# Regrouping the lead-in of a fused linear-attention and gated feed-forward kernel

## The chip, the cores and the metric

The kernel runs on one core of one Trainium2 chip. The metric is the device time of one execution in microseconds (us); less is better. The time before is 211.69 us, the median of 7 runs, from 210.19 to 416.03 us; the six runs other than the longest lie between 210.19 and 212.92 us.

## The reference

Linear attention with a decay per head, in blocks of 64 positions, and after it a feed-forward layer whose gate is `h * cos(h)`:

```
q, k, v: (4, 8, 768, 64) f32     lam: (8,)     w_in: (512, 2048)     w_out: (2048, 512)
for each block b of 64 positions (sl):
    intra = (q[sl] @ k[sl].T * Dmask) @ v[sl]          # Dmask = lam ** (i - j), 0 above the diagonal
    inter = (q[sl] * lam ** (pos + 1)) @ kv_state
    out[sl] = intra + inter
    kv_state = lam ** 64 * kv_state + (k[sl] * lam ** (63 - pos)).T @ v[sl]
x = out as (3072, 512)            # tokens by heads * head_dim
h = x @ w_in
g = h * cos(h)
return g @ w_out                  # (3072, 512) f32
```

## The kernel before

The 3072 tokens are 24 blocks of 128, numbered n from 0. They are gathered into eight feed-forward tiles of 4, 2, 2, 2, 2, 4, 4 and 4 blocks (`TILES`). The decay is put into q and k/v as powers of lam beforehand (`q_sp`, `v_sp`, `q_scale`, `v_scale`), so that a block needs only a masked product and a running state.

**The first tile, blocks 0 to 3, is the lead-in.** It has a code path of its own, `add_span(x)`, for x = 0 and 1; each x stands for 256 positions of one batch entry, two tokens to a partition. For each x the loads bring 512 KB of q, k and v (`sp_f`). The eight heads are handled in two halves, hp = 0 and 1. For each half: q and v are scaled to bf16 (`prep`, line 475), k is cast (`prep_k`, line 479), q and k are transposed on TensorE (line 486) and evicted (line 489), the scores are formed (line 497) and masked (line 502), and the values are multiplied in (line 523). Between the two blocks of one x lies the state: `update` (line 510) forms k times v, `update_out` (line 514) brings it to `kv_bd`, `carried` (line 529) adds it to the second block, and `values_out` (line 537) evicts a block into `xT`, the transposed input of the feed-forward.

**A feed-forward tile** (`add_ffn`) has 16 chunks f of 128 hidden columns. `hidden` (line 591) does four matmuls a chunk into `ps_h`, ScalarE takes the cosine (line 597), VectorE multiplies (line 603) into `g`. For tile 0 the first `SPLIT` chunks are done in two halves, blocks 0 and 1 and then blocks 2 and 3, so that work can begin before the last `xT` is there. Then `project` (line 631) multiplies `g` by w_out: for each block j four groups of four matmuls of 512 columns, called by their first chunk f0 = 0, 4, 8 and 12; the group f0 needs quarter f0/4 of w_out. The finished block is evicted (line 643) and stored (lines 650 and 652).

**The later blocks** come through `prepare` (scaling at lines 323 and 331, cast of k at line 327), transposes on TensorE (line 351) for blocks 4 and 5 and by DMA (line 357) from block 6 on, `add_scores` (line 384) and `add_stretch` (state at line 412, values at lines 424 and 428). Their work is laid between the groups of the feed-forward of the tile before.

**The weights** are cast from f32 to bf16 by DMAs that GpSimd issues (line 264): w_in in pieces of `W_IN` chunks, w_out in four quarters. `ORDER` gives the order of all loads: q, k and v of x = 0 and 1, then w_in, then w_out, then the loads of block 4 and on. The first w_in piece is issued when k of x = 1 has landed, and the load of q of block 4 waits until the third quarter of w_out has landed:

```python
ORDER = "q0 k0 q1 k1 v0 v1 i0 i1 i2 i3 i4 o0 o1 o2 o3"
W_IN = [3, 3, 4, 3, 3]
        deps = [kept[-3 if soft else -2]] if at and (names[at - 1][0] in "io") != soft else []
```

**The order on every engine is fixed when the program is built.** A planner (`Planner.order`) plays the tasks through with a cost for each and picks, engine by engine, the task that can start first and, of those, the one of lowest priority number. The instructions are then written out in order of planned start; an engine runs them strictly in that order, and where the chip is later than the plan it waits. The costs that matter here: 0.5 us on SyncE for the issue of a load, 0.8 us on GpSimd for that of a weight piece, 2.6 us of DMA for four chunks of weights, 1.5 us for a load of `sp_f`, 1.1 us for one of a later block, and 1.6 to 2.8 us from the end of a transfer until its data may be used:

```python
    SETUP = {"POOL": 5.6, "DVE": 5.6, "ACT": 7.3, "SP": 1.3}
    MM = lambda cols, n=1: n * (cols / 2400.0 + 0.0025)
        _, w_t[which, c] = dma("POOL", 2.6 * part, 0.8, emit, ...)
                    t = pl.add("PE", MM(width, U4), ..., project, pr, banks=0 if f0 else 1)
```

Where the plan leaves TensorE idle in the lead-in, `keep_awake` writes out matmuls on a blank tile (line 706); it stops at the chunk `lead_end = hid[2 * SPLIT]`.

Of the kernel before, what the change touches and what calls it, by code (L numbers as in the profile page):

```python
# [18 lines left out]
SPANS = 2  # L19
DMA_FROM = 6  # L20
TILES = [4, 2, 2, 2, 2, 4, 4, 4]
SPLIT = 4
BANKS = 7
LAG = 2
ATT = 0.95
ALONE = [2, 3, 4]

QV = [[("DVE", "POOL"), ("DVE", "POOL")], [("DVE", "POOL"), ("DVE", "POOL")]]
OUTS = [{"qT": ("DVE", "DVE"), "kT": ("ACT", "ACT")}, {"qT": ("ACT", "ACT"), "kT": ("ACT", "ACT")}]
V_PRIO = {"POOL": -1.7, "DVE": 0.0}  # L30
LATE = 30.0
ORDER = "q0 k0 q1 k1 v0 v1 i0 i1 i2 i3 i4 o0 o1 o2 o3"

W_IN = [3, 3, 4, 3, 3]


class Task:
# [101 lines left out]
def kernel(  # L139
# [10 lines left out]
    nc = tc.nc  # L150
    B, H, S, D = q.shape
    P = 128
    NB = S // P
    NBLK = B * NB
    NP = H // 2
# [3 lines left out]
    KF = D_FF // P  # L159
# [33 lines left out]
    for i in range(2):  # L193
        m = mask_sp[i * D:(i + 1) * D].rearrange("u k (s t) -> u k s t", s=2)
# [24 lines left out]
    v_sp = consts.tile([P, H, 2], F32)  # L219
# [179 lines left out]
    def add_stretch(pr):  # L399
# [59 lines left out]
        for x, y in zip(chain, chain[1:]):  # L459
            x.then = y  # L460
            y.deps.append(x)

    def add_span(x):
# [3 lines left out]
        us = {"DVE": 0.69, "POOL": 1.1}  # L467
# [4 lines left out]
        place = lambda t, hp: t[:, :, cut[hp]].rearrange("u s h d -> u h s d")  # L472

        def prep(_, name, hp, e):
            vec[e].tensor_mul(place(L[name], hp), live[name + "_f", "sp", x][:, cut[hp]],  # L475
                              (q_sp if name == "q" else v_sp)[:, cut[hp]].unsqueeze(3).to_broadcast([P, 4, 2, D]))

        def prep_k(_, hp):
            nc.scalar.copy(place(L["k"], hp), live["k_f", "sp", x][:, cut[hp]])

        def transposes(task, name, hp):
            t = L["t", name, hp] = bank(task.bank[0], [P, 2, 2, P], BF16, "ps_t")
# [50 lines left out]
        def values_out(_, c, e, pairs):  # L533
# [3 lines left out]
            (nc.scalar.copy if e == "ACT" else nc.vector.tensor_copy)(  # L537
                live["xT", 0][:, pairs, n * P:(n + 1) * P], L["o"][c][:, pairs])

        so, kt, v_t = [[], []], [], []  # L540
        for hp in range(2):
            eq, ev = QV[x][hp]
            a = pl.add(eq, us[eq], [load_t["q_f", "sp", x]], partial(prep, name="q", hp=hp, e=eq), pa(-0.9 + 0.1 * hp))
            kt.append(pl.add("ACT", 0.61, [load_t["k_f", "sp", x]], partial(prep_k, hp=hp), pa(-0.9 + 0.1 * hp)))
            v_t.append(pl.add(ev, us[ev], [load_t["v_f", "sp", x]], partial(prep, name="v", hp=hp, e=ev), pa(V_PRIO[ev] + 0.1 * hp)))
            outs = []
            for name, src in (("qT", a), ("kT", kt[hp])):
                e = OUTS[x][name][hp]
                t = pl.add("PE", MM(P, 4), [src], partial(transposes, name=name, hp=hp), pa(-0.5 + 0.1 * hp), banks=1)
                outs.append(pl.add(e, 0.58 if e == "ACT" else 0.42, [t], partial(transposes_out, name=name, hp=hp, e=e), pa(-0.5 + 0.1 * hp)))  # L550
                t.bank_frees = [[outs[-1]]]
            s1 = pl.add("PE", 0.42, outs, partial(scores, hp=hp), pa(0.1 + 0.1 * hp), banks=2)
# [19 lines left out]
    h_last, o_last = {}, {}  # L572
    hid = []

    def add_ffn(i):
# [4 lines left out]
        for f in range(KF):  # L580
            gate[f] = []
            blocks = [(0, 2), (2, 4)] if i == 0 and f < SPLIT else [(0, nb)]
            for b0, b1 in blocks:
# [16 lines left out]
                def gated(_, f=f, at=at, n=n):  # L600
                    if ("g", i) not in live:
# [4 lines left out]
                h = pl.add("PE", MM(n, 4), [x for m in range(n0 + b0, n0 + b1) for x in Vo[m]] + [w_t["in", next(c for c in range(len(W_IN)) if f < sum(W_IN[:c + 1]))]],  # L606
                           hidden, pr, banks=1)
                a = pl.add("ACT", 0.21 + n * 0.000833, [h], cosine, pr, get="cos")
                d = pl.add("DVE", 0.12 + n * 0.00104, [a] + ([o_last[i - 2]] if i >= 2 else []), gated, pr)
# [8 lines left out]
        for j in range(nb):  # L618
# [3 lines left out]
            for piece, part in enumerate(pieces):  # L622
                width = part.stop - part.start
                for f0 in range(0, KF, U4):
                    pr = begins[i + 1] + (j + f0 / KF) * nxt / nb + piece

                    def project(task, j=j, f0=f0, piece=piece, part=part, width=width):
                        if f0 == 0:
                            live["f", i, j, piece] = bank(task.bank[0], [P, DM], F32, "ps_f")
                        for f in range(f0, f0 + U4):  # L630
                            nc.tensor.matmul(live["f", i, j, piece][:, :width], lhsT=live["g", i][:, f, j * P:(j + 1) * P],  # L631
                                             rhs=w_out_sb[:, f, part], start=(f == 0), stop=(f == KF - 1))
# [35 lines left out]
    for at, name in enumerate(names):  # L668
        which, n = name[0], int(name[1:])
        soft = which in "io"  # L670
        deps = [kept[-3 if soft else -2]] if at and (names[at - 1][0] in "io") != soft else []
        if soft:
            kept.append(add_w({"i": "in", "o": "out"}[which], n, at, deps))
        elif n < SPANS and at < 15:
# [70 lines left out]
```

## The time and the profile before

| what | value |
|---|---|
| median of 7 runs | 211.69 us |
| the profiled execution, its own time | 211.13 us |
| span of the profile, first to last instruction | 209.4 us |
| TensorE busy (matmuls) | 199.0 us, 95% of the span |
| VectorE, ScalarE, GpSimd busy | 120.3, 112.1, 63.6 us |
| mean granted TensorE clock | 0.992 |
| first matmul of the feed-forward (line 591) | at 16.99 us |
| first matmul of the projection (line 631) | at 32.90 us |
| first transpose of block 4 (line 351) | at 39.20 us |

In the profile's lines PE is TensorE (matmul), PEld its weight loads, DVE is VectorE, ACT is ScalarE, POOL is GpSimd, SP is SyncE; a q behind the name is the engine's sequencer, which waits and issues DMAs. A line of the timeline gives start, duration, engine, line of the program, operation, `out<-in` with its shape and count, and in brackets the idle time of the engine just before it and what ended that.

### The profile page before, as it was taken

The numbers are of one execution on the slowest core, as the hardware profiler recorded it, in microseconds if no ns is written. First come the engines' busy times: TensorE is split into PE (matmuls) and PEld (weight loads), VectorE is DVE, ScalarE is ACT, GpSimd is POOL, SyncE is SP. The second block draws the span as 40 slices with busy tenths as digits, with TensorE's granted clock in tenths as the row PEclk, the third lists the DMA queues.
The fourth block names the chain that finished last, engine by engine and source line by source line (L and its number), as shares of the span: only waits on it lengthen the run. The fifth ranks groups of instructions, "written<-read, shape, count | busy, mean of one in ns | idle before, by whom it ended". The sixth has DMA issues, their size and how long they took to land.

```text
span 209.4 us, 4536 instructions
## 1 busy us (share of the span) xinstructions
PE 199.0 (95%) x1786; PEld 116.8 (56%) x1813; DVE 120.3 (57%) x220; ACT 112.1 (54%) x207; POOL 63.6 (30%) x82
## 2 busy tenths in 40 slices
PE   6769999999999999999999999999999999999993
PEld 6448544447856758766664555445445444444462
DVE  3695773274975849676849797838533444333000
ACT  5967875325917737656545745654554555355120
POOL 4099000164335726363636554610000000000000
PEclk9996999999999999999999999999999999999999
DMA  4999999998999999999999999931101110111112
GB/s 127 347 240 142 185 206 221 209 241 227 211 215 210 277 191 263 199 248 203 267 247 213 246 260 231 229 106 48 50 1 49 53 52 0 50 50 50 53 65 85
DMA packets 96229, 34.38 MB, mean 164 GB/s; under 512 B 82256, under 2 KB 93264, under 8 KB 96208
## 3 DMA queue, kind: packets, MB, share of 16 engines
q1 hardware_dynamic: 91312, 29.77, 60.8%
q0 software_dynamic: 4752, 4.19, 13.0%
q8 instruction: 14, 0.23, 0.4%
q10 hardware_dynamic: 144, 0.13, 0.2%
q14 instruction: 7, 0.06, 0.1%
HBM read 27.27 MB, written 6.29 MB: 160 GB/s over the span
## 4 chain that ended last, share of the span: by engine, by line
PE 70%; DMA 18%; POOL 5%; SPq 3%; issue 2%; DVE 1%; ACT 0%; POOLq 0%; ACTq 0%
PE ps_f L631 33%; PE ps_h L591 29%; DMA w_out_sb<-in_moe_w_out_dram 7%; DMA v_f<-in_v_dram 4%; DMA sp_f<-in_k_dram 3%; SPq L264 3%; PE ps_s L384 2%; DMA q_f<-in_q_dram 2%; DMA qkT<-qk 2%; POOL v_sp L475 2%; PE ps_o L424 2%; PE ps_o L428 2%; POOL w_in_sb L264 2%; PE ps_kv L412 1%; POOL w_out_sb L264 1%
## 5 line engine op out<-in xcount | busy, mean ns | idle before, releaser
L597 ACT ACTIVATE cos<-ps_h,halfpi 128x256 f32<-128x256 f32 (+1 forms) x132 | 72.9, 571 | 50.9 <-PE ps_h L591 50.1
L603 DVE TENSOR_TENSOR g<-ps_h,cos 128x256 bf16<-128x256 f32 (+1 forms) x132 | 70.8, 545 | 49.3 <-ACT cos L597 47.0
L591 PE MATMUL ps_h<-xT,w_in_sb 128*128 128x256 bf16 (+1 forms) x523 | 92.9, 323 | 0.2
L631 PE MATMUL ps_f<-w_out_sb,g 128*128 128x512 bf16 (+1 forms) x380 | 90.9, 370 | 1.5 <-issue 0.8
L591 PEld LDWEIGHTS <-w_in_sb 128*128 128x128 bf16 x528 | 51.9, 99 | 34.9 <-issue 0.2
L631 PEld LDWEIGHTS <-g 128*128 128x128 bf16 x400 | 38.0, 98 | 39.0
L323 POOL TENSOR_TENSOR qk<-q_f,q_scale 128x512 bf16<-128x512 f32 x19 | 19.9, 1060 | 48.1 <-DMA q_f<-in_q_dram 44.7
L643 ACT COPY o_sb<-ps_f 128x512 f32<-128x512 f32 (+1 forms) x24 | 13.9, 577 | 25.5 <-PE ps_f L631 25.4
L390 DVE TENSOR_TENSOR s_m<-ps_s,mask 128x512 bf16<-128x512 f32 x40 | 25.6, 683 | 0.6 <-PE ps_s L384 0.4
L331 POOL TENSOR_TENSOR v_s<-v_f,v_scale 128x512 bf16<-128x512 f32 x19 | 19.6, 1044 | 13.8 <-DMA v_f<-in_v_dram 12.6
L417 DVE CAST kv_bd<-ps_kv 64x512 bf16<-64x512 f32 x16 | 11.0, 688 | 9.5 <-PE ps_kv L412 9.2
L435 ACT CAST xT<-ps_o 128x512 bf16<-128x512 f32 x20 | 10.7, 588 | 10.1 <-PE ps_o L428 9.6
L327 POOL CAST qk<-k_f 128x512 bf16<-128x512 f32 x18 | 11.0, 613 | 3.7 <-DMA k_f<-in_k_dram 3.4
L428 PE MATMUL ps_o<-s_m,v_s 128*64 128x128 bf16 x160 | 7.6, 219 | 0.0
L424 PE MATMUL ps_o<-qkT,kv_bd 128*64 128x128 bf16 x144 | 7.1, 220 | 0.0
L384 PE MATMUL ps_s<-qkT 64*128 64x128 bf16 x160 | 6.7, 218 | 0.4 <-DMA qkT<-qk 0.2
L706 PE MATMUL ps_idle<-blank,ident 128*128 128x128 bf16 (+1 forms) x43 | 5.1, 309 | 1.7 <-POOL ident masks.py:199 1.6
L643 DVE COPY o_sb<-ps_f 128x256 f32<-128x256 f32 x1 | 0.4, 425 | 10.7 <-PE ps_f L631 10.7
L264 POOL DMA_DIRECT2D w_in_sb<-in_moe_w_in_dram x5 | 4.0, 803 | 6.9 <-DMA sp_f<-in_k_dram 6.9
L384 PEld LDWEIGHTS <-qkT 64*128 64x128 bf16 x160 | 4.6, 94 | 2.1 <-DVE s_m L390 0.4
L428 PEld LDWEIGHTS <-v_s 128*64 128x64 bf16 x160 | 5.5, 110 | 0.0
L706 PEld LDWEIGHTS <-ident 128*128 128x128 bf16 x45 | 4.5, 142 | 1.7 <-POOL ident masks.py:199 1.6
(60 smaller groups left out, 71.2 us busy)
## 6 DMA issues: line engine op xcount, KB each, us to landing
q_f<-in_q_dram SPq DMA_DIRECT2D x20, 256.0 KB, 3.6
k_f<-in_k_dram SPq DMA_DIRECT2D x20, 256.0 KB, 4.1
v_f<-in_v_dram SPq DMA_DIRECT2D x20, 256.0 KB, 4.4
out_dram<-o_sb SPq DMA_DIRECT2D x19, 256.0 KB, 2.0
w_out_sb<-in_moe_w_out_dram POOLq DMA_DIRECT2D x4, 512.0 KB, 13.0
w_in_sb<-in_moe_w_in_dram POOLq DMA_DIRECT2D x4, 384.0 KB, 6.5
out_dram<-o_sb SPq DMA_DIRECT2D x9, 128.0 KB, 3.2
sp_f<-in_q_dram SPq DMA_DIRECT2D x2, 512.0 KB, 5.3
```

The source lines that it names most:

```text
L264: i = queue.dma_start(out=o, in_=x)
L323: vec[e].tensor_mul(live["qk", n][:, 0], live.pop(("q_f", n)), q_scale[:, c, :].unsqueeze(2).to_broadcast([P, H, D]))
L331: vec[e].tensor_mul(live["v_s", n], live.pop(("v_f", n)), v_scale[:, c, :].unsqueeze(2).to_broadcast([P, H, D]))
L384: nc.tensor.matmul(live["s", n][i][:, p, :], lhsT=live["qkT", n][h, 1, p, :], rhs=live["qkT", n][h, 0, p, :], start=True, stop=True)
L390: nc.vector.tensor_mul(live["s_m", n][:, i], live["s", n][i], mask.unsqueeze(1).to_broadcast([P, NP, P]))
L424: nc.tensor.matmul(o[h, p, :], lhsT=kv_bd[(slot - 1) % NK][:, s, p, h], rhs=live["qkT", n][:, 0, p, :], start=(p == 0), stop=False, skip_g ...
L428: nc.tensor.matmul(o[h, p, :], lhsT=live["v_s", n][:, 2 * p + i, :], rhs=live["s_m", n][:, i, p, :], start=(p == 0 and c == 0), stop=True, ...
L591: nc.tensor.matmul(t[:, :n], lhsT=w_in_sb[:, kd, f * P:(f + 1) * P], rhs=live["xT", i][:, kd, at], start=(kd == 0), stop=(kd == KD - 1))
L597: nc.scalar.activation(c[:, :n], live["h", i, f, at.start][:, :n], AF.Sin, bias=halfpi)
L603: nc.vector.tensor_mul(live["g", i][:, f, at], live.pop(("h", i, f, at.start))[:, :n], live.pop(("c", i, f, at.start))[:, :n])
L631: nc.tensor.matmul(live["f", i, j, piece][:, :width], lhsT=live["g", i][:, f, j * P:(j + 1) * P], rhs=w_out_sb[:, f, part], start=(f == 0) ...
L643: (nc.scalar.copy if eng == "ACT" else nc.vector.tensor_copy)(o[:, :width], live["f", i, j, piece][:, :width])
```

## The change

Five things change, all in the lead-in.

1. `SPLIT` goes from 4 to 3: three chunks of tile 0 are done in halves.
2. `W_IN` goes from 3, 3, 4, 3, 3 to 3, 5, 4, 4, and `ORDER` names four w_in pieces instead of five.
3. The scaling and casting of the lead-in is divided anew (`QKV` gives engines for q, k and v of each x and half). For x = 0 the cast of k for heads 0 to 3 goes from ScalarE to GpSimd. For x = 1 the scaling of q for heads 4 to 7 goes from VectorE to GpSimd, and that of v for heads 4 to 7 goes from GpSimd to ScalarE, where it is eight multiplications of 128x64 by a scalar of each partition, planned at 1.4 us and held behind the last eviction of kT.
4. Both halves of `update_out` go to ScalarE (the first update had one of them on VectorE). `values_out` of the second block is no longer divided between ScalarE and VectorE; whole blocks go to ScalarE or VectorE. `update` of x = 1 now comes behind `carried` of x = 0 on TensorE, and `hidden` of tile 0 from chunk 1 on behind `carried` of x = 1.
5. The group f0 = 12 of block 0's projection gets a later priority, between the groups f0 = 8 and f0 = 12 of block 1.

```diff
-SPLIT = 4
+SPLIT = 3
-QV = [[("DVE", "POOL"), ("DVE", "POOL")], [("DVE", "POOL"), ("DVE", "POOL")]]
+QKV = [[("DVE", "POOL", "POOL"), ("DVE", "ACT", "POOL")], [("DVE", "ACT", "POOL"), ("POOL", "ACT", "ACT")]]
-V_PRIO = {"POOL": -1.7, "DVE": 0.0}
+V_PRIO = {"POOL": -1.7, "ACT": 1.0}
-ORDER = "q0 k0 q1 k1 v0 v1 i0 i1 i2 i3 i4 o0 o1 o2 o3"
-W_IN = [3, 3, 4, 3, 3]
+ORDER = "q0 k0 q1 k1 v0 v1 i0 i1 i2 i3 o0 o1 o2 o3"
+W_IN = [3, 5, 4, 4]
...
         def prep(_, name, hp, e):
+            if e == "ACT":
+                for h in range(4 * hp, 4 * hp + 4):
+                    for s in range(2):
+                        nc.scalar.mul(L[name][:, s, h, :], live[name + "_f", "sp", x][:, h, s, :], v_sp[:, h, s:s + 1])
+                return
...
-        def prep_k(_, hp):
-            nc.scalar.copy(place(L["k"], hp), live["k_f", "sp", x][:, cut[hp]])
+        def prep_k(_, hp, e):
+            (nc.scalar.copy if e == "ACT" else nc.gpsimd.tensor_copy)(place(L["k"], hp), live["k_f", "sp", x][:, cut[hp]])
...
-            before = Uo_sp.get((1, 0), []) if c else Uo_sp.get((x - 1, 0), [])
+            before = Uo_sp.get((1, 0), []) if c else Uo_sp.get((x - 1, 0), []) + [carry.get(x - 1)]
...
-                           for h, e in zip(halves, ("ACT", "ACT" if c else "DVE"))]
+                           for h, e in zip(halves, ("ACT", "ACT"))]
...
-        Vo[2 * x] = [pl.add("ACT", 0.6, [v1], partial(values_out, c=0, e="ACT", pairs=slice(0, NP)), pv(0.3))]
-        Vo[2 * x + 1] = [pl.add(e, 0.38, [second], partial(values_out, c=1, e=e, pairs=pairs), -1200.0)
-                         for e, pairs in (("ACT", slice(0, 2)), ("DVE", slice(2, 4)))]
+        carry[x] = second
+        for c, e, src in ((0, "DVE" if x else "ACT", v1), (1, "ACT" if x else "DVE", second)):
+            Vo[2 * x + c] = [pl.add(e, 0.6 if e == "ACT" else 0.69, [src], partial(values_out, c=c, e=e), -1200.0 if c else pv(0.3))]
...
-                h = pl.add("PE", MM(n, 4), [x for m in range(n0 + b0, n0 + b1) for x in Vo[m]] + [...],
+                h = pl.add("PE", MM(n, 4), ([carry[1]] if i == 0 and f else []) + [x for m in range(n0 + b0, n0 + b1) for x in Vo[m]] + [...],
...
                     pr = begins[i + 1] + (j + f0 / KF) * nxt / nb + piece
+                    if i == 0 and j == 0 and f0 == KF - U4:
+                        pr = begins[1] + (1.9 - U4 / KF) * nxt / nb
...
+    v_act.deps.append(last_out[1])
```

More of the change, by code (lines that the diff above doesn't have):

```diff
@@ L461, in add_stretch @@
             y.deps.append(x)
+    v_act = None
     def add_span(x):
@@ L466, in add_span @@
         cut = [slice(4 * hp, 4 * hp + 4) for hp in range(2)]
-        us = {"DVE": 0.69, "POOL": 1.1}
+        us = {"DVE": 0.69, "POOL": 1.1, "ACT": 1.4}
         vec = {"DVE": nc.vector, "POOL": nc.gpsimd}
@@ L531, in carried, with values_out @@
                                  start=False, stop=True, skip_group_check=True)
-        def values_out(_, c, e, pairs):
+        def values_out(_, c, e):
             if ("xT", 0) not in live:
@@ L537, in values_out @@
             (nc.scalar.copy if e == "ACT" else nc.vector.tensor_copy)(
-                live["xT", 0][:, pairs, n * P:(n + 1) * P], L["o"][c][:, pairs])
+                live["xT", 0][:, :, n * P:(n + 1) * P], L["o"][c])
         so, kt, v_t = [[], []], [], []
         for hp in range(2):
-            eq, ev = QV[x][hp]
+            eq, ek, ev = QKV[x][hp]
             a = pl.add(eq, us[eq], [load_t["q_f", "sp", x]], partial(prep, name="q", hp=hp, e=eq), pa(-0.9 + 0.1 * hp))
-            kt.append(pl.add("ACT", 0.61, [load_t["k_f", "sp", x]], partial(prep_k, hp=hp), pa(-0.9 + 0.1 * hp)))
+            kt.append(pl.add(ek, 0.61, [load_t["k_f", "sp", x]], partial(prep_k, hp=hp, e=ek), pa(-0.9 + 0.1 * hp)))
             v_t.append(pl.add(ev, us[ev], [load_t["v_f", "sp", x]], partial(prep, name="v", hp=hp, e=ev), pa(V_PRIO[ev] + 0.1 * hp)))
+            if ev == "ACT":
+                nonlocal v_act
+                v_act = v_t[-1]
             outs = []
@@ L551, in add_span @@
                 t.bank_frees = [[outs[-1]]]
+            last_out[x] = outs[-1]
             s1 = pl.add("PE", 0.42, outs, partial(scores, hp=hp), pa(0.1 + 0.1 * hp), banks=2)
@@ L572 @@
     h_last, o_last = {}, {}
+    last_out, carry = {}, {}
     hid = []
@@ L604, in gated @@
                                          live.pop(("c", i, f, at.start))[:, :n])
-                h = pl.add("PE", MM(n, 4), [x for m in range(n0 + b0, n0 + b1) for x in Vo[m]] + [w_t["in", next(c for c in range(len(W_IN)) if f < sum(W_IN[:c + 1]))]],
+                h = pl.add("PE", MM(n, 4), ([carry[1]] if i == 0 and f else []) + [x for m in range(n0 + b0, n0 + b1) for x in Vo[m]] + [w_t["in", next(c for c in range(len(W_IN)) if f < sum(W_IN[:c + 1]))]],
                            hidden, pr, banks=1)
@@ L673 @@
             kept.append(add_w({"i": "in", "o": "out"}[which], n, at, deps))
-        elif n < SPANS and at < 15:
+        elif n < SPANS and at < 14:
             kept.append(add_span_load(which + "_f", src[which], n, at - 40, deps))
```

## The prediction

> **What bounds the kernel now.** I read the slices of the page first, then the chain that ended last, then the lead-in by engine. The slices (5.2 us each):
>
> ```profile
> PE   6769999999999999999999999999999999999993
> PEclk9996999999999999999999999999999999999999
> DMA  4999999998999999999999999931101110111112
> ```
>
> TensorE is full from the fourth slice to the end, so time can be won only ahead of it, in its clock, or in waits inside. The stretches of the lead-in (length, busy PE, PEld, DVE, ACT, POOL, granted clock, DMA share, GB/s) show two faults:
>
> ```profile
> 16.00:17.00 1.00, 1.00 (x33) 0.83 (x34) 0.54 (x2) 0.70 (x2) 1.00 (x3) 0.50 0.99 151
> 17.00:18.00 1.00, 1.00 (x8) 0.76 (x7) 0.43 (x1) 0.62 (x2) 1.00 (x2) 0.50 0.35 42
> 18.00:19.00 1.00, 1.00 (x9) 0.82 (x7) 0.51 (x2) 0.53 (x2) 1.00 (x2) 0.50 0.80 97
> ```
>
> The clock is halved (by the clock's records from 15.88 to 19.29 us, a loss of 1.71 us of TensorE work), and the weight transfers run dry at 17 us (42 GB/s against some 200 around it), because the third w_in piece is issued only when GpSimd has scaled v. The chain (start, duration, what) follows that:
>
> ```profile
> 10.40 1.23 POOL w_in_sb L264 x2
> ...
> 12.10 4.06 POOL v_sp L475 x4
> 16.15 2.23 POOL w_in_sb L264 x3
> 18.39 1.44 POOL w_out_sb L264 x2
> 19.83 13.86 DMA w_out_sb<-in_moe_w_out_dram
> ...
> 33.71 4.72 DMA q_f<-in_q_dram
> ...
> 38.45 0.70 DVE qk L323
> ...
> 39.20 0.40 PE ps_t L351 x4
> ```
>
> The third quarter of w_out lands at 33.69, only then q of block 4 is loaded, and its first transpose starts at 39.20. TensorE had come there by its own path too: its idle time before 39.20 is 0.1 us. So two paths end within a few tenths of each other: TensorE's own work since the lead-in, and the stream of weights. Gaining on one alone buys little. The timeline there:
>
> ```profile
> 32.90 5.73 PEld L631 LDWEIGHTS <-g 128*128 128x128 bf16 x28
> 38.45 0.69 DVE L323 TENSOR_TENSOR qk<-q_f,q_scale 128x512 bf16<-128x512 f32 x1 [4.66 <-DMA q_f<-in_q_dram]
> ```
>
> Twenty-eight weight loads, so seven groups of the projection, lie ahead of that transpose. Order is fixed in the program; remember the seven.
>
> **Part 1, the division of the lead-in.** GpSimd gains a cast of k (0.61 us, row of line 327) and a scaling of q (1.06, row of line 475). Both fit its idle time:
>
> ```profile
> 10.40 1.69 POOL L264 DMA_DIRECT2D w_in_sb<-in_moe_w_in_dram  x2 [6.90 <-DMA sp_f<-in_k_dram]
> ```
>
> k and q of their x land at 7.03 and 8.59, so both are done by 9.7, before the 10.10 that the issue waits for: nothing on the path. Without that cover the w_in issue would slip by up to 1.67 us. Taking the fourth scaling of v off GpSimd lets the third w_in issue start at 15.1 instead of 16.09.
>
> ScalarE takes that scaling as eight pieces of 64 columns; no row shows one. From below: activations of 16 columns from SBUF start 0.12 apart (lines 215 and 220), 48 more columns at 0.00084 (0.69 less 0.47 over 256 columns of the cosine) make 0.16, so 1.3 us. From above: cosines of 256 columns start 0.45 apart, less 192 columns gives 0.29, so 2.3 us. The first rows are nearest (SBUF source, short): 1.4 us. The Trainium skill (ScalarE: Activation LUTs, What ACT_TABLE_LOAD costs) gives 186 ns plus 0.833 ns a column, 93 ns more for a scalar of each partition, and 93 ns of overlap: an estimate of 0.24 us each, 1.9 in all, which this trace neither confirms nor excludes; it would bring the lead gain below from 0.3 to about -0.1 and, as will be seen, leave the sum where it is. v of x = 1 lands at 13.07, ScalarE is free at 12.95, so the pieces end at 14.5 (14.4 to 15.4). Behind them on ScalarE waits the first `kv_bd`, which ran at 14.56.
>
> `kv_bd` and the second block's `xT` went through two engines, but one after the other (the DVE half at 14.96 was released by the ACT half; 16.40 likewise). Two halves on ScalarE at 0.375 each take 0.75 us instead of 0.83; a whole `xT` takes 0.59 (ScalarE) or 0.69 (VectorE, the nearest row being the 64x512 cast of line 417) instead of 0.83. Chain: `kv_bd` 14.6 to 15.35, `carried` 15.45, `xT` on VectorE 15.9 to 16.6, first feed-forward matmul 16.65 instead of 16.99. The lead gain is 0.3 us; with pieces of 2.3 us it is -0.4, with shorter waits at most 0.5. The new ties of `update` and `hidden` to `carried` cost nothing: in the trace one chunk, then `carried` at 17.82, then the rest already stand in that order. If `kv_bd` came late, all of `hidden` from chunk 1 on would stand behind it, its delay in full.
>
> **Part 2, SPLIT.** One chunk goes as 512 columns instead of 2 x 256: 4 matmuls of 0.2157 against 8 of 0.1091, 0.01 us. Nothing.
>
> **Part 3, the pieces of w_in.** One issue of 0.75 us less. The first piece lands at 15.72 as now. A chunk takes 0.637 us when the stream is full (1.91 us for the three that land at 17.63), so the second piece with five lands at 18.9. Chunk 3, now in it, is needed at about 20 (at 19.2 with a full clock): free, at worst 0.3. The third piece now queues up before the stream runs dry. From 18.9 to the landing L of the third quarter of w_out are 20 chunks: at 0.62 (second quarter, 2.49 us for four) L = 31.3; at 0.677 (now, from third w_in piece to third quarter: 12.19 us for 18), and 19.1 for the start, L = 32.6. I take 0.65, L = 31.9 instead of 33.69.
>
> **Part 4, the last quarter.** The eviction of block 0's projection starts at 38.29, six groups and not four after 32.90. So two groups of block 1 already stood ahead of f0 = 12, and now it is three. That quarter lands at 36.35 and its group started at 37.23: no wait to remove. Price 0; it shields what an earlier TensorE would run into.
>
> **What comes of it.** q of block 4 lands 4.74 us after L (33.69 to 38.43), and its transpose follows 0.77 later: L + 5.51 = 37.4. But L enters the plan as well: working the planner's times by hand, block 4's transpose is ready at 37.17 in the plan of before, inside the seventh group (planned start 31.6, 0.863 each: as the trace has it), and at 35.37 in the new plan, inside the fifth. So only five groups stand ahead of it: TensorE is there at 32.90 - 0.3 + 5 x 0.863 = 36.9, and waits 0.5 us for the load. The two groups still owed cost 1.73. Against before: 37.4 + 1.73 - 39.20 = -0.07 us. The lead gain is swallowed by a wait, and the earlier stream by the place of the transpose. Bounds: at L = 31.3 TensorE's own path decides, 36.9 + 1.73 - 39.20 = -0.57; at L = 32.6 it is +0.64. Later waits (0.3 before the second scores at 44.11) I leave as they are.
>
> Span 209.4, so 209.3; the profiled execution took 211.13 us, 0.56 less than the median of the runs, so the change is put on the median: 211.69 - 0.07 = 211.6, own range 211.1 to 212.4. The clock does not enter: with 1.71 us back TensorE only waits longer for block 4. The Trainium skill (TensorE: Matmul & The Clock Gate, Part 1) says that the gate judges in windows of 3.4 us that run free of the kernel's start, so the cold stretch may move or vanish from run to run; by that rule TensorE's own path could be 1.7 us shorter in either kernel, while the sum by the load stays.
>
> **Rivals.** A, the gain comes through: later tasks shift the plan so that seven groups stay ahead, and the clock stays at 1.00. TensorE is there at 38.93 - 0.3 - 1.71 = 36.9, the load at 37.4: 39.20 - 37.4 = 1.8 us gained, 2.3 with L = 31.4, so 209.4 to 209.9. For it: the 0.50 rows and the slack in GpSimd. Against: TensorE's work in the judged stretch hardly changes, and my hand count gives five. Chance 0.20, of which 0.12 is over 1%.
>
> B, slower: the stream is no faster, because larger pieces or the transfers beside them slow it, and L stays at 33.69. Then the transpose starts at 39.20 with two groups still owed: +1.73, 213.4. It decides from L = 32.0 on, and gives 1% from 34.1. For it: the quarters now take up to 2.66 us each, with a full queue. Against: the empty second at 17 us. Chance 0.13, of which 0.08 is over 1% with other waits added.
>
> C, the division does not act as it says: two engines that write one tile go one after the other, as `kv_bd` and `xT` did. ScalarE's pieces are planned at 12.9, before GpSimd's part of the same v at 13.5, so GpSimd ends at 15.55 to 16.5 instead of 15.15; the lead is 0.6 later instead of 0.3 earlier, TensorE is at block 4 at 37.8, and 37.8 + 1.73 - 39.20 = +0.3, 212.0. Against: both pairs also read one PSUM bank, which the new pairs do not. Chance 0.10.
>
> The forecast has 0.57. About 1% (2.1 us) is what a measurement of this kernel can tell from no change. Faster by over 1%: 0.12 from A and 0.01 of the forecast; slower: 0.08 from B and 0.01 from C; within: 0.78. The range reaches from most of A to B: 209.5 to 213.5.
>
> **What would show it.** The third quarter of w_out lands near 31.9; 20 instead of 28 weight loads of `ps_f` stand ahead of the first transpose of block 4, and TensorE idles about 0.5 us there; the DMA row at 17 us is near 200 GB/s; eight ScalarE pieces begin at 13.1 and take 1.4; the first feed-forward matmul starts near 16.65. I am wrong if that transpose comes after seven groups, if L is past 33, or if the first feed-forward matmul comes before 16.

## The result, and the profile after

The changed kernel takes 213.09 us, the median of 27 runs, against 211.21 us for the kernel before on the same chip (64 runs). The ratio is 1.0077, with a 95% interval from 1.0058 to 1.0097; ratios here leave out runs more than 1.5% above the fastest of their kernel, the medians do not, so a ratio is not exactly the quotient of two medians. Two later comparisons on other chips gave 1.0137 [1.0091, 1.0184] and 1.0110 [1.0083, 1.0137]. All three intervals lie above 1: the change makes the kernel about 1% slower, where the forecast was no change.

The profiled execution of after took 211.29 us, the quickest of its runs; its span is 209.6 us. The slices:

```profile
PE   6869999899999999999999999999999999999993
PEclk9999999999999999999999999999999999999999
DMA  4999999997999999998999999941101110111112
```

The clock was full in the lead-in of this execution, and its span is no shorter than before's 209.4. The stretches of the lead-in (the columns are those of before) show the dry second at 17 us gone, 199 GB/s in place of 42:

```profile
16.00:17.00 1.00, 0.85 (x36) 0.58 (x34) 0.71 (x2) 0.75 (x2) 1.00 (x2) 1.00 1.03 177
17.00:18.00 1.00, 0.87 (x10) 0.83 (x11) 0.58 (x1) 0.63 (x3) 1.00 (x2) 1.00 1.25 199
18.00:19.00 1.00, 1.00 (x11) 0.79 (x9) 0.42 (x1) 1.00 (x4) 1.00 (x3) 1.00 1.12 151
```

The chain of the lead-in (start, duration, what), with GpSimd's new scaling of q ahead of the first w_in issue and the third w_in issue at 15.12:

```profile
8.72 1.47 POOL q_sp L482
...
10.38 1.22 POOL w_in_sb L264 x2
...
15.12 1.49 POOL w_in_sb L264 x2
16.61 1.45 POOL w_out_sb L264 x2
18.06 14.80 DMA w_out_sb<-in_moe_w_out_dram
```

The third quarter of w_out lands at 32.87 (before 33.69). The timeline at block 4's first transpose has 20 weight loads ahead of it, five groups, and TensorE idle for 0.65 us:

```profile
32.01 4.00 PEld L645 LDWEIGHTS <-g 128*128 128x128 bf16 x20
37.15 0.40 PE L351 MATMUL ps_t<-ident,qk 128*128 128x128 bf16 x4 [0.65 <-DVE qk L323]
```

And ScalarE's eight pieces, with `kv_bd` right behind them:

```profile
13.15 2.02 ACT L480 ACTIVATE v_sp<-sp_f,v_sp 128x64 bf16<-128x64 f32 x8 [0.21 <-DMA sp_f<-in_v_dram]
15.07 0.73 ACT L521 CAST kv_bd<-ps_kv 64x256 bf16<-64x256 f32 x2
```

Up to 40 us this is nearly what was foretold. In this quickest execution TensorE has no wait at any scores of the later blocks, and the span is 0.2 us over before's; in a typical one there is a loss, and it lies further back. One row for the stretch from 35 to 100 us, in before, in after (a later execution of it, span 211.6) and in the best kernel of the experiments, in that order; the second column is TensorE's busy time in these 65 us:

```profile
35.00:100.00 65.00, 63.68 (x669) 42.95 (x678) 42.74 (x89) 35.27 (x76) 28.90 (x32) 1.00 1.05 225
```

```profile
35.00:100.00 65.00, 61.99 (x653) 41.51 (x663) 41.67 (x87) 34.26 (x73) 29.81 (x33) 1.00 1.08 225
```

```profile
35.00:100.00 65.00, 65.00 (x686) 43.75 (x685) 43.62 (x92) 36.11 (x78) 30.09 (x33) 1.00 1.07 228
```

TensorE idles 1.3 us there in before, 3.0 in after and not at all in the third, so 1.7 of the 2.2 us by which after's span is longer are idle time in this stretch. The largest single wait in that execution of after is at the second scores of a pair (blocks 12 and 13), which want a tile that a DMA transpose brings:

```profile
87.04 0.40 PE L384 MATMUL ps_s<-qkT 64*128 64x128 bf16 x8
88.74 0.40 PE L384 MATMUL ps_s<-qkT 64*128 64x128 bf16 x8 [1.30 <-DMA qkT<-qk]
```

In before the same two scores ran as one group of 16 matmuls without a wait between them:

```profile
88.91 0.62 PE L384 MATMUL ps_s<-qkT 64*128 64x128 bf16 x16
```

Block 13's tile landed at 88.77 in before and at 88.69 here. So the tile is as late as ever, and TensorE comes for it almost 2 us sooner, with more of its other work still to do.

### The profile page after: what moved, and what is told of

It reads as the page before. It is cut to its first block, busy times and chain, and to the rows that moved or that the text cites. A ratio compares the mean times of both kernels' runs of the same rounds, so it can differ in the third digit from the quotient of the medians.

```text
span 209.6 us, 4528 instructions
## 1 busy us (share of the span) xinstructions
PE 198.4 (95%) x1783; PEld 115.6 (55%) x1808; DVE 119.3 (57%) x216; ACT 113.3 (54%) x213; POOL 63.7 (30%) x82
## 4 chain that ended last, share of the span: by engine, by line
PE 74%; DMA 16%; POOL 5%; issue 1%; SPq 1%; ACT 0%; DVE 0%; POOLq 0%; ACTq 0%
PE ps_f L645 35%; PE ps_h L603 31%; DMA w_out_sb<-in_moe_w_out_dram 7%; DMA sp_f<-in_q_dram 3%; PE ps_s L384 3%; DMA qkT<-qk 2%; DMA v_f<-in_v_dram 2%; DMA q_f<-in_q_dram 2%; PE ps_o L428 2%; PE ps_o L424 2%; POOL v_sp L482 1%; PE ps_kv L412 1%; POOL w_in_sb L264 1%; SPq L264 1%; POOL q_sp L482 1%
## 5 line engine op out<-in xcount | busy, mean ns | idle before, releaser
L609 ACT ACTIVATE cos<-ps_h,halfpi 128x256 f32<-128x256 f32 (+1 forms) x131 | 73.0, 574 | 57.7 <-PE ps_h L603 57.4
L603 PE MATMUL ps_h<-xT,w_in_sb 128*128 128x256 bf16 (+1 forms) x518 | 94.2, 322 | 0.6 <-DVE xT L544 0.3
L645 PE MATMUL ps_f<-w_out_sb,g 128*128 128x512 bf16 (+1 forms) x382 | 92.0, 370 | 1.6 <-issue 1.0
L603 PEld LDWEIGHTS <-w_in_sb 128*128 128x128 bf16 x524 | 50.8, 98 | 36.9 <-issue 0.4
L645 PEld LDWEIGHTS <-g 128*128 128x128 bf16 x400 | 38.2, 98 | 37.4
L721 PE MATMUL ps_idle<-blank,ident 128*128 128x128 bf16 (+1 forms) x43 | 5.6, 320 | 1.7 <-POOL ident masks.py:199 1.6
L509 DVE TENSOR_TENSOR s_m_sp<-ps_s,mask_sp 128x512 bf16<-128x512 f32 x8 | 5.1, 685 | 0.8 <-PE ps_s L504 0.7
```

The lines of the kernel that those rows point to most:

```text
L603: nc.tensor.matmul(t[:, :n], lhsT=w_in_sb[:, kd, f * P:(f + 1) * P], rhs=live["xT", i][:, kd, at], start=(kd == 0), stop=(kd == KD - 1))
L609: nc.scalar.activation(c[:, :n], live["h", i, f, at.start][:, :n], AF.Sin, bias=halfpi)
```

## The experiments

Each was compared with the kernel before on the same chip. The first four were made when three theories stood: P, that two groups of projection still owed behind block 4's first transpose are the loss; L, that the lead is later and the rest follows; W, that larger w_in pieces slow the stream.

**After again.** No edit.

> The changed kernel once more, for a second profile: the first one (211.29 us) was the fastest of its runs, 1.8 under their median. Theory P (place: five groups of the projection ahead of block 4's first transpose, so TensorE waits for the load): 0.8% slower than before, and in a typical profile TensorE idles 1 us or more just before that transpose, with the third quarter of w_out landing at 33 us or later. Theory L (lead: ScalarE's pieces and the longer chain through kv_bd make the lead-in later): the same time, but the idle time lies before the first feed-forward matmul, at 17.5 us or later, and little is lost at block 4. Theory W (the larger w_in pieces): TensorE waits for chunk 3 near 20 us.

Ratio 1.0137; span 211.5. The third quarter landed at 32.84 and block 4's transpose started at 37.22, as in the first profile, but the execution was 2 us longer. So the loss is not in the lead-in: the eviction of block 2 comes 0.24 us later than in before's profile, and those from block 11 on 2.09 us later throughout (in between the two orders differ).

**After with seven groups.** The planner is told that loads of blocks 4 and 5 are ready later, so block 4's transpose moves back behind seven groups:

```diff
- dma("SP", 1.1, 0.5, emit, prio, deps, get=name)
+ dma("SP", 1.1, 0.5, emit, prio, deps, get=name, lat=3.7 if n < 6 else 1.9)
```

> The changed kernel with one number of the plan altered: the loads of blocks 4 and 5 are planned 1.8 us later (lat 3.7 instead of 1.9), so that seven groups of the projection stand ahead of block 4's first transpose again, as in the kernel before. Nothing else differs, and no work is added. P: the loss is gone, ratio to before 0.993 to 1.000 (211.2 or a little less). L and W: nothing changes, ratio 1.006 to 1.010.

Ratio 1.0105 [1.0067, 1.0142]. Block 4's transpose started at 38.87 with no wait, and 0.3% of the 1.4% came back. P explains a small part at most.

**Before with five groups.** The same place in before, moved the other way: `lat=0.1 if n < 6 else 1.9`.

> The kernel before with the reverse: the loads of blocks 4 and 5 are planned 1.8 us earlier (lat 0.1), so that only five groups stand ahead of block 4's first transpose, and the weights and the lead-in are as before. P: two groups are owed at 39.2 us, so 1.73 us slower, ratio 1.006 to 1.010. L and W: ratio 1.000.

Ratio 1.0079 [1.0048, 1.0111], as P said. The timeline has the price, a wait for the third quarter (35.19) and then for block 4:

```profile
35.23 2.75 PE L631 MATMUL ps_f<-w_out_sb,g 128*128 128x512 bf16 x11 [0.29 <-DMA w_out_sb<-in_moe_w_out_dram]
39.40 0.40 PE L351 MATMUL ps_t<-ident,qk 128*128 128x128 bf16 x4 [1.42 <-DVE qk L323]
```

So the two groups do cost when the third quarter comes as late as in before (though the plan moved there too, and in the table below the later block 15 stands over block 4, 207.8 against 206.4); in after it comes sooner, and they nearly pay for themselves, as the prediction reckoned.

**The lead-in alone, with seven groups.** After with `W_IN = [3, 3, 4, 3, 3]`, five pieces in `ORDER`, and `lat=2.8 if n < 6 else 1.9`.

> The new division of the lead-in, SPLIT 3 and the late last quarter, but w_in in pieces of 3, 3, 4, 3, 3 as before, and seven groups ahead of block 4's first transpose (lat 2.8). L: slower by the whole 0.8%, ratio 1.006 to 1.010. P: ratio 0.995 to 1.002. W: ratio 0.995 to 1.002 too; against the run with seven groups and the new pieces it tells what the pieces do: W has that one slower by 0.6% or more, P has them equal within 0.3%.

Ratio 1.0214 [1.0175, 1.0254], outside every theory. The table of TensorE's waits from 40 to 105 us (total, times, longest) names the place that all three had left out:

```profile
PE ps_s L384 <- DMA qkT<-qk: 3.7, 6, 1.1
```

**A new theory, S.** Every engine's order is fixed by the planner. In after its plan has the w_out quarters, and so the later blocks, sooner: the scores of block 13 are planned at 84.4 us instead of 87.2. Their tile comes at the end of a stream of loads, stores and transposes that fills the DMA row of the slices until some 140 us. It landed at 86.7, 88.6 and 88.7 in three executions of after, against 88.8 in before. TensorE then stands at scores with an instruction it cannot start, and everything behind it waits. If so, the span is the largest over all blocks of (landing of the block's tile) + (TensorE work that stands behind its scores), or the same for block 4's transpose, plus a tail. The work behind is summed from the planner's own costs for the matmuls in their order. For block 13 it is 115.9 us in before and 118.5 in after: three groups of 0.863 more.

| kernel | block 4's transpose + work behind | block 13's tile + work behind | largest sum (block) | span | ratio to before |
|---|---|---|---|---|---|
| before | 39.2 + 165.3 | 88.8 + 115.9 | 205.4 (15) | 209.4 | 1 |
| after, first profile | 37.2 + 167.0 | 86.7 + 118.5 | 205.2 (17) | 209.6 | 1.0077 |
| after again | 37.2 + 167.0 | 88.6 + 118.5 | 207.1 (13) | 211.5 | 1.0137 |
| after, seven groups | 38.9 + 165.3 | 87.9 + 118.5 | 206.4 (19) | 210.8 | 1.0105 |
| before, five groups | 39.4 + 167.0 | 90.5 + 116.7 | 207.8 (15) | 211.8 | 1.0079 |
| lead alone, seven | 39.1 + 165.3 | 92.1 + 118.0 | 210.2 (13) | 214.6 | 1.0214 |
| after, scores later | 37.8 + 167.0 | 90.8 + 115.9 | 208.7 (21) | 212.6 | 1.0007 |
| after, seven, scores later | 39.6 + 165.3 | 89.7 + 115.0 | 206.6 (21) | 210.5 | 0.9959 |
| after, transposes first | 37.3 + 167.0 | 88.6 + 119.3 | 207.9 (13) | 212.3 | 1.0054 |
| before, scores sooner | 39.5 + 165.3 | 88.9 + 119.3 | 208.5 (19) | 212.7 | 1.0185 |
| after, third time | 37.5 + 167.0 | 88.7 + 118.5 | 207.2 (13) | 211.6 | 1.0110 |
| after, seven, later, second time | 40.3 + 165.3 | 89.1 + 115.0 | 205.5 (4) | 210.0 | 1.0019 |
| before, scores later | 39.3 + 165.3 | 88.4 + 115.4 | 205.0 (19) | 209.2 | 0.9993 |
| pieces alone, seven | 38.0 + 165.3 | 88.1 + 118.5 | 207.5 (15) | 211.6 | 1.0123 |
| pieces, seven, scores later | 38.0 + 165.3 | 87.2 + 115.0 | 204.0 (21) | 207.9 | 0.9955 |
| lead, seven, scores later | 39.5 + 165.3 | 88.8 + 115.9 | 204.8 (4) | 209.5 | 1.0025 |

In all 16 profiles the span is the largest sum plus 3.9 to 4.8 us. Sums closer than that 0.9 us do not tell which block binds, and the block with the largest sum is not always one at which TensorE waits. Sums and spans are of one execution each, ratios of all that were compared. The sum explains a span once the tiles have landed; the test is what happens when only the order is changed.

**After with the scores later.** One number of the planner: a DMA transpose is believed to be ready 5.0 us after its end.

```diff
-            T[n].lat = 3.0
+            T[n].lat = 5.0
```

> The kernel after with one number of its planner changed: a DMA transpose from block 6 on is believed to be ready 5.0 us after it ends instead of 3.0, so TensorE's order puts the scores of blocks 6 to 15 up to three groups later (planned TensorE work behind the scores of block 13: 115.9 us, as in before, instead of 118.5), while block 4's first transpose keeps its early place (167.0 us behind it, after five groups of projection). The order of SyncE changes a little with it. Theory S (after loses where TensorE stands at scores whose DMA-transposed qkT has not landed, because they stand too early in its order; latest landing plus the work behind it, plus 4.2 to 4.5 us, gives the span): the largest sum falls from 207.1 (block 13, 88.6 + 118.5) to 204.2 (block 4's transpose, 37.2 + 167.0) or 204.7 (block 15, some 98.5 + 106.2), span 208.5 to 209.3, time 0.995 to 1.003 of before; no wait over 0.5 us at the scores from block 6 to 15. Theory P (the place of block 4's transpose is what costs): unchanged by this edit, 1.010 to 1.014. Theory L (the lead and the load of w_out are later): unchanged, 1.010 to 1.014. Theory Q (the order of loads and transposes on SyncE is the cause, not TensorE's): 1.000 to 1.005 here, and the run e2_transposes_first alone gives the same.

Ratio 1.0007 [0.9970, 1.0044]: the loss is gone, as S said, with lead-in, pieces and five groups untouched. On this chip before itself took 213.58 us, and block 22's tile landed at 139.6 to 142.0 us in the four profiles made there, against 136.8 in before's first profile and 137.6 in after's. So the spans are longer than foretold, and the profile still waits 1.1 us for tiles between 105 and 140 us. After without the edit was not run on this chip.

**After with seven groups and the scores later.** Both edits.

> The kernel after with both orders moved: seven groups of projection ahead of block 4's first transpose (165.3 us of TensorE work behind it, as in before) and the scores of blocks 6 to 15 later by the same 5.0 us (115.0 us behind those of block 13). Theory S: the largest sum is block 15's, some 97.5 + 106.6 = 204.1, or block 4's, 38.2 + 165.3 = 203.5; span 207.9 to 208.8, time 0.993 to 1.000 of before, the candidate to beat it. Theory P: 0.997 to 1.005, as the seven groups alone should have brought. Theory L: 1.010, as the seven groups alone measured. Theory Q: 1.000 to 1.010; its order still has a load between the transposes of blocks 12 and 13.

Ratio 0.9959 [0.9922, 0.9996], within S's range.

**After with the transposes first on SyncE.** In after's plan a load of q stands between the DMA transposes of blocks 12 and 13; this takes it away and leaves TensorE's places nearly as they are:

```diff
                 issue_t["q_f", n + LAG].deps.append(head)
+                if n % 2:
+                    issue_t["q_f", n - 1 + LAG].deps.append(head)
```

> The kernel after with one dependency more in its planner: the load of q for an even block waits for the issue of both DMA transposes ahead of it, so that on SyncE no load stands between the transposes of blocks 12 and 13, or 14 and 15, as in before. TensorE's places stay nearly those of after (119.3 us behind the scores of block 13, 107.9 behind those of block 15). Theory Q: block 13's transposed tile lands 1.5 to 3 us sooner than the 88.6 of after, the time falls to 1.000 to 1.005 of before. Theory S: the tile lands 1 to 2 us sooner, but 0.8 us more of work stands behind it, and the blocks 8, 9 and 15 come next with 206.1 to 206.3; span 210.3 to 211.2, time 1.006 to 1.012. Theories P and L: 1.010 to 1.014.

Ratio 1.0054 [1.0019, 1.0089], just below S's range and just above Q's. The step that both had foretold did not show: block 13's tile landed at 88.57, as after's 88.58 on the other chip, where 1 to 3 us less were expected. The two transposes side by side took 4.39 us to issue:

```profile
82.06 4.39 SPq L357 DMA_TRANSPOSE qkT<-qk  x2
```

After itself did not run on this chip, so a share of Q is not excluded by this run.

**Before with the scores sooner.** The reverse: in before only, `T[n].lat = 1.0`.

> The kernel before with the same number of the planner moved the other way: a DMA transpose is believed to be ready 1.0 us after it ends instead of 3.0, so that the scores of blocks 6 to 15 stand two to three groups earlier (119.3 us of work behind those of block 13, as in after), with the lead, the w_in pieces, the seven groups ahead of block 4's transpose and the order of transposes and loads on SyncE (blocks 12, 13 and 14, 15 side by side) as in before. Theory S: block 13's sum rises from 204.6 to about 207 or 208, span 211 to 212.5, time 1.008 to 1.017 of before, with waits of 0.5 us and more at the scores of blocks 7 to 15. Theories P, L and Q: nothing they name is touched, 0.998 to 1.003.

Ratio 1.0185 [1.0121, 1.0250], from six runs of 214.36 to 218.52 us against 211.22 to 214.94 for before. This kernel has nothing of the change but the places of the scores and of what the planner hangs on them: values and states on TensorE, their evictions, and on SyncE a few loads and stores. Its transposes of blocks 12 and 13 stand side by side on SyncE as in before, and it loses as much as after or more. Nor do its tiles come later: those of blocks 6 to 13 landed at 54.7, 57.4, 66.1, 66.9, 76.8, 77.6, 88.1 and 88.9 us, in before's first profile at 54.6, 57.4, 66.0, 66.9, 76.7, 77.6, 87.8 and 88.8. TensorE comes to them sooner and stands. Its timeline at blocks 6 and 7, and behind it before's, with both in one group:

```profile
55.77 0.40 PE L384 MATMUL ps_s<-qkT 64*128 64x128 bf16 x8
57.45 0.40 PE L384 MATMUL ps_s<-qkT 64*128 64x128 bf16 x8 [1.29 <-DMA qkT<-qk]
```

```profile
57.23 0.62 PE L384 MATMUL ps_s<-qkT 64*128 64x128 bf16 x16
```

With the first run of this group, that shows from both sides that a plan with sooner scores is enough for a loss of this size.

**After a third time, and the two parts in turn.** The next four shared one chip.

> The kernel after as it is, beside the three others on one chip, so that what the edits regain is read on one chip. Theory S: span 210.5 to 212.5, 1.008 to 1.014 of before, with waits of 0.5 to 1 us at the scores between blocks 6 and 15. Theory G (the parts of the change cost something by themselves, besides the order): the same.

Ratio 1.0110 [1.0083, 1.0137], as expected; its wait at block 13 is the one shown above.

> The kernel after with seven groups of projection ahead of block 4's first transpose and the scores of blocks 6 to 15 later, a second time, beside after on one chip. Theory S: the sums that bind are block 15's (99.1 + 106.6 = 205.7 in its first profile) and block 4's (204.9); 0.993 to 0.999 of before, 0.012 to 0.018 less than after. Theory G: 0.999 to 1.004.

Ratio 1.0019 [0.9998, 1.0041]. The 0.9% against after on the same chip is again the order's (both places together; the seven groups alone had brought 0.3%), less than S said, and the kernel is not below before: a miss. Waits at the scores there are none. What binds is block 4's transpose at 40.27, behind 27 recorded matmuls without a wait, because TensorE came late out of the lead-in. The stretches (the seventh column is the granted clock) and the timeline:

```profile
14.00:16.00 2.00, 1.32 (x42) 0.92 (x42) 1.17 (x2) 1.96 (x8) 2.00 (x4) 0.69 1.23 204
16.00:18.00 2.00, 2.00 (x39) 1.46 (x38) 1.19 (x2) 1.15 (x3) 2.00 (x3) 0.50 1.17 204
18.00:20.00 2.00, 2.00 (x14) 1.56 (x12) 0.62 (x2) 1.27 (x3) 1.58 (x3) 0.50 1.20 191
```

```profile
34.21 6.22 PE L645 MATMUL ps_f<-w_out_sb,g 128*128 128x512 bf16 x27
40.27 0.39 PE L351 MATMUL ps_t<-ident,qk 128*128 128x128 bf16 x4
```

**Before with the scores later** (`T[n].lat = 5.0` in before alone).

> The kernel before with the scores of blocks 6 to 15 later by the same 5.0 us (115.4 us of TensorE work behind those of block 13, 104.9 behind block 15's, 144.8 behind block 7's), seven groups ahead of block 4's first transpose as it has them, nothing else of the change. Theory S: block 15's sum falls from 205.4 to 203.7 and block 4's stays at 204.5 (39.2 + 165.3), so at most 0.9 us is gained: 0.995 to 1.000 of before; the place of the scores explains most of what the kernel with seven groups and later scores gained. If the shorter load of w_out of the change matters by itself, the kernel with seven groups and later scores is 0.5 to 1.0 us below this one (its block 4 starts no sooner, so theory S in its narrow form says no difference over 0.5 us).

Ratio 0.9993 [0.9968, 1.0019]. The later place alone gives before nothing: block 4's transpose (204.6) and block 19 (205.0) hold it.

**The pieces alone, with seven groups.** Before with what the prediction calls parts 3 and 4, and the place of block 4 kept:

```diff
-ORDER = "q0 k0 q1 k1 v0 v1 i0 i1 i2 i3 i4 o0 o1 o2 o3"
+ORDER = "q0 k0 q1 k1 v0 v1 i0 i1 i2 i3 o0 o1 o2 o3"
-W_IN = [3, 3, 4, 3, 3]
+W_IN = [3, 5, 4, 4]
- dma("SP", 1.1, 0.5, emit, prio, deps, get=name)
+ dma("SP", 1.1, 0.5, emit, prio, deps, get=name, lat=3.3 if n < 6 else 1.9)
...
+                    if i == 0 and j == 0 and f0 == KF - U4:
+                        pr = begins[1] + (1.9 - U4 / KF) * nxt / nb
```

> The kernel before with only the third part of the change, w_in in pieces of 3, 5, 4, 4 and the last quarter of w_out left for later, and block 4's place put back to seven groups; the lead-in work stays where before has it. Its plan puts the scores of block 13 where after has them (118.5 us behind them, 107.9 behind block 15's). Theory S: latest sum about 88.2 + 118.5 = 206.7, span 210.8 to 211.5, 1.007 to 1.013 of before, although nothing of the lead is changed. Theory G with the lead at fault (work spread over GpSimd and ScalarE): 0.998 to 1.002. Theory G with the pieces at fault: 1.008 to 1.013, but then the kernel with seven groups and later scores, which has the pieces too, is not below before.

Ratio 1.0123 [1.0095, 1.0151], with before's lead-in: all of after's loss, from the plan's earlier scores, though block 4's transpose is 1.2 us ahead of before's (38.03). TensorE waits three times, at the scores of blocks 7, 13 and 15:

```profile
PE ps_s L384 <- DMA qkT<-qk: 1.9, 3, 0.8
```

**Each part alone, the order put right.** Open was which part is worth anything once the scores stand later. These two shared a further chip. First the pieces, the kernel just shown with `T[n].lat = 5.0`:

> The kernel before with the third part of the change alone (w_in in pieces of 3, 5, 4, 4, the last quarter of w_out left for later), seven groups ahead of block 4's first transpose and the scores of blocks 6 to 15 later by the 5.0 us; 115.0 us of work behind the scores of block 13, 106.2 behind block 15's. Theory S: block 4's first transpose starts near 38.0 as it did without the later scores, 38.0 + 165.3 = 203.3; blocks 13 and 15 give 88.5 + 115.0 = 203.5 and 98.8 + 106.2 = 205.0 at most; span 207.5 to 209.3, 0.992 to 1.001 of before and 0.011 to 0.020 below the same kernel with the scores sooner. If the lead-in's spreading is what keeps the kernel with seven groups and later scores at before's time (first feed-forward matmul 17.2 to 17.4 there, 16.6 here), this one is under 0.997. If the stream of loads sets a floor of its own, 0.998 to 1.002.

Ratio 0.9955 [0.9928, 0.9981], median 210.32 us against 211.31. Its interval lies below before in the one comparison that it had (after with seven groups and later scores had two, and was below before in one). Taken from two chips, it is 1.7% below the same kernel with the scores sooner. Block 13's tile landed at 87.23, TensorE came to it at 88.58 and had both tiles:

```profile
88.58 0.62 PE L384 MATMUL ps_s<-qkT 64*128 64x128 bf16 x16
```

Then the lead-in, `W_IN` and `ORDER` of before, with `lat=2.8 if n < 6 else 1.9` and `T[n].lat = 5.0`. Its expectation says that the first tile's projections are in before's order; the later place of the last quarter in fact stayed in it, as in the run of the lead alone.

> The lead-in part of the change alone: w_in in before's five pieces and all of the first tile's projections in before's order, with the work spread over GpSimd and ScalarE as after has it, seven groups ahead of block 4's first transpose and the scores of blocks 6 to 15 later (115.9 us of work behind those of block 13). Theory S: the same kernel with the scores sooner stood at 1.021 with block 13's tile at 92.1; with some 2 us less work behind that tile, 92 + 115.9 = 207.9 if the tile is as late again, 88.5 + 115.9 = 204.4 if it is not: 1.000 to 1.016. The lead as the prediction priced it (0.3 us gained): 0.996 to 1.000. The lead as after's profile showed it (first feed-forward matmul 0.1 to 0.4 us later): 1.000 to 1.004.

Ratio 1.0025 [0.9993, 1.0057]. The order accounts for most of the 2.1% of its twin; what is left, 0.25% with an interval that includes none, is what the third alternative said of a later lead.

## Why the prediction was wrong, point by point

**The step that failed** is one short sentence in the sum: "Later waits (0.3 before the second scores at 44.11) I leave as they are." (The trace has 0.15 us of idle TensorE there, not 0.3.) The prediction saw that an earlier w_out enters the plan and worked out what the plan does to block 4. It did not go on to ask what the same shift does to every later block. The edits stand in the lead-in, but the plan moves the scores of blocks 6 to 19 forward: by its own costs 1.3 to 3.9 us more work stands behind them than in before, 2.6 us for blocks 6 to 13. (The new lead-in does part of this without the new pieces: 118.0 us behind block 13's scores in the run of the lead alone.) The tiles they need did not come sooner by as much. In place of waits that stay as they are, the largest sum rose from 205.4 to 207.1 and 207.2 in the second and third profiles of after, and the span from 209.4 to 211.5 and 211.6. The next wait was visible in before, at the second scores of blocks 14 and 15:

```profile
98.84 0.40 PE L384 MATMUL ps_s<-qkT 64*128 64x128 bf16 x8 [0.24 <-DMA qkT<-qk]
```

Block 15's tile landed at 98.79 there, and block 15's sum is the largest, 205.4. The two ends that were compared, TensorE and the weights at block 4, stand at 204.5, so neither was the last.

**The parts ahead of that were nearly right.** Five groups, counted by hand: 20 weight loads. TensorE at block 4 with a wait: 0.65 us against 0.5. Its transpose at 37.15 against 37.4, so by the prediction's own sum 37.15 + 1.73 - 39.20 = -0.3 us, and yet the kernel is slower. None of the signs that the prediction had named for being wrong appeared.

**L** was 32.87, 32.84 and 32.78, not 31.9, and past the bound of 32.6. The second piece landed at 19.46 instead of 18.9, and the 20 chunks after it took 0.67 us each instead of 0.65. The load of block 4 made up for it: it landed 3.5, 3.6 and 4.0 us after L, not 4.74. That two misses cancel at block 4 is luck.

**The lead** was priced at 0.3 us gained. In the kernels whose clock was full there, the first feed-forward matmul starts at 16.64 to 16.71 with before's lead-in (four profiles) and at 17.09 to 17.13 with the spread one (four): 0.4 us lost. The mis-sized term is ScalarE's eight pieces, 2.02 us and not 1.4, so that `kv_bd` starts at 15.07 instead of 14.56; from there to the first feed-forward matmul it took 2.06 us, where the prediction has 2.05. The other 0.3 us is in what it was set against: 16.99 comes from a profile of before with half the clock from 15.89 on. The estimate of 1.9 from the Trainium skill (ScalarE: Activation LUTs, What ACT_TABLE_LOAD costs) was the better one; the trace agrees with it at 0.25 us a piece against 0.24.

**The clock.** "The clock does not enter" held where the load decides: after's block 4 started at 37.15 with a full clock, and at 37.22 and 37.54 with a cold stretch (half the clock) from 15.3 to 18.7 us. For before it is less clear. Beside the first four experiments its spans were 208.6 to 210.2 us, median 208.9, with a full clock (eight runs), 208.6, 208.7 and 210.1 with a mean clock of 0.99, and 210.3 with 0.98; beside the last two the medians were 209.5 (19 runs) and 210.4 (three, at 0.99). It fails once nothing else binds: in after with seven groups and later scores a cold stretch of 6.8 us put the first projection at 34.21, where after's first profile, with the same lead-in and a full clock, has 32.01. That cold stretches begin at 15.9, 15.3, 17.1 and 14.8 in different executions, or not at all, and last 3.41 us or twice that, agrees with the Trainium skill's free-running windows of 3.4 us (TensorE: Matmul & The Clock Gate, Part 1).

Cold executions are commoner with the new lead-in: 72 of the 106 runs compared that have it show a mean clock under 0.996, and 31 of the 119 with before's. That is not the loss: in the runs with a full clock alone, after's median spans are 211.7 and 211.25 us on two chips (two runs each), against 208.9 and 209.0 for before there (8 and 20 runs).

**The rivals.** A asked for seven groups ahead of block 4. The run that gave after seven groups was still 1.05% slower, so the gain was not behind that place. B, the slower rival, had the right sign and nearly the size by the wrong mechanism: it decides from L = 32.0 on, but its loss needs q of block 4 to take 4.74 us from L, and it took 3.5 to 4.0; that its number came out is luck. C, the two engines one after the other, was not seen: ScalarE's pieces ran from 13.15 to 15.17 while GpSimd scaled its three parts from 12.07 to 15.12.

**What stays open** is why the stream, 0.9 us ahead at L, has lost that lead by block 13 in two of after's three profiles and kept it in the pieces kernel; tiles of one and the same kernel landed up to 2 us apart there. Open too is how much of after's own loss comes from the order on SyncE that moves with the scores.

## What to carry to other kernels

Where a planner fixes every engine's order, an edit that makes its plan earlier than the chip can be may be a loss, as here: it moves instructions ahead of work that could have run, and one that is early stops its engine until its input is there. For a fixed order, add for every transfer the time it lands and the engine's work that stands behind its first user; the largest of these sums bounds the end, and a change is worth at most what it takes off that one until the next. When two parts of a change lean on one wrong belief, correct the belief before judging the parts: here it hid that one of them gains 0.45% (interval 0.2 to 0.7%, one comparison) and the other nothing that could be measured.

## What the runs showed of the hardware

The time that SyncE needs to issue a DMA varies within one execution. In the third run of after the 18 transposes, all of one shape, took 1.24 to 3.36 us to issue, median 1.29; the longest is block 13's, with 0.57 for the load of q ahead of it. What stretches an issue no run here isolates.

```profile
82.61 0.57 SPq L264 DMA_DIRECT2D q_f<-in_q_dram  x1
83.32 3.36 SPq L357 DMA_TRANSPOSE qkT<-qk  x1
```

GpSimd's scaling of q in the lead-in took 1.47 us in all ten profiles that have it, where the same shape took 1.02 us each in after's three scalings of v at 12.07. In after's first profile it began at 8.72, while VectorE scaled the other half of q (8.60 to 9.29); whether that is the reason no run here isolates.
